# Turning the activated rows by DMA instead of TensorE, and a changed order for the last token tiles, in a fused attention and two-layer mixture kernel

## The chip, the cores and the metric

The kernel runs on one core of a Trainium2 chip. Five engines work in parallel, each through its own instructions in a fixed order: TensorE (PE, matmuls and transposes; its weight loads are listed apart as PEld), VectorE (DVE), ScalarE (ACT), GpSimd (POOL), and SyncE (SP), which here only issues DMAs. PE writes to PSUM; DVE and ACT read PSUM, POOL does not. The metric is the time of one execution in microseconds on the device; less is better.

## What is computed

Three stages, one after the other, on 1152 tokens (2 sequences of 576) of 512 features:

```python
scores = q @ k.T / 8                        # 2 x 8 heads, 576 x 576
mask = scores >= (32nd largest of the row)  # others to -1e9
x = softmax(scores) @ v                     # -> [1152, 512]
xn = x / rms(x) * rms_g
x = (silu(xn @ w_gate) * (xn @ w_val)) @ w_out         # d_ff 1536
logits = x @ r_gate; e = argmax(logits); gate = softmax(logits)[e]
# token i takes the next free slot of expert e (288 slots each, 8 experts)
out[i] = gate * (relu(x[i] @ w1[e]) @ w2[e])           # F2 = 1024
```

## The kernel before

**Number format.** Matmuls of the second and third stage run in f16 with both operands split into an upper and a lower half (value = hi + lo); each product is three matmuls: hi·hi, hi·lo, lo·hi.

**Tiles.** Tokens go in nine tiles of 128 (`t` = 0 to 8), heads in pairs, so there are 36 pairs of work `p = 4t + hp`. For each pair `scores` makes the scores (L308), `topk` finds the 32nd largest with four MAX8 and three MATCH_REPLACE8 per head on DVE (L322, L331, L334), `weights` makes the softmax's numerators (ACT L350, L356, POOL L351) and `values` turns them and multiplies by v (L374, L382). After a tile's four pairs come `norm` (the rms norm, result `xn` as two f16 halves), `moe1` (the first feed-forward layer) and `dispatch` (routing and scatter of the row).

**moe1(t).** It runs over three groups g of 512 hidden features. Two products of 12 matmuls (L448) give gate and value; from these ACT and, for tiles 1 to 7, POOL make the activated rows `h` [128 tokens x 512] in f32 (L461 to L468). `turned(g, h)` then turns h: four transposes on PE into a PSUM buffer (L434), and `halves` splits that into the tile `hT[g]`, the upper half by ACT (L420) and the lower by DVE (L421). Groups 0 and 1 are turned after the first row chunk of the next group, group 2 after the fourth of the twelve row chunks (f = 0 to 11) of the down product (L473), whose chunks f = 8 to 11 read `hT[2]`.

**dispatch(t).** y, the layer's result, is turned (L492), copied by ACT (L494) and multiplied by the router's weights (L505). DVE, ACT and POOL find the expert and the slot (`ev` is the engine of four small steps: DVE for tile 8, else POOL). ACT squares y for a scale (L499) with the buffer `yd` as scratch; `yd` (one buffer) also takes the row that an indirect DMA of POOL writes to `disp` in DRAM (L568).

**Experts.** Weights (16 matrices of 2 MB) are loaded by SP (L722), sized (`size`, ACT L735) and split into halves (`convert`: ACT L760, DVE L762 and L765). Rows of an expert are fetched from `disp` by a transposing DMA (`gather`, L776) with their notes (L789). Expert 0 begins with the first 128 slots ("a") and takes up to 48 more ("b") later. Three weight loads stand behind the last of the first gathers on SP.

**Order.** The program is written by an outer loop of slots: each pair is 14 slots, and generators (`at`, `ahead`) are advanced at given slots. Scores, weights, values and norm have a raised priority; moe1 and dispatch have none. A scheduler then fixes each engine's order from priorities and modelled times, so each engine's order is static at run time. `after(t, engine)` puts the instructions traced in its block behind a remembered instruction, on that instruction's engine only. Two buffer pools matter: `wraw` (four buffers of 4 KB per partition, for raw weights and a row of zeros, all before 165 us), and `pm` (three PSUM banks, shared by the products and by the turned rows).

Of the kernel before, what the change touches and what calls it, by code (L numbers as in the profile page):

```python
# [8 lines left out]
F32 = mybir.dt.float32  # L9
F32R = mybir.dt.float32r  # L10
F16 = mybir.dt.float16
BF16 = mybir.dt.bfloat16
I32 = mybir.dt.int32
U32 = mybir.dt.uint32
AF = mybir.ActivationFunctionType
OP = mybir.AluOpType
PSUM = bass.MemoryType.PSUM

P = 128
B, H, S, D = 2, 8, 576, 64  # L20
N = B * S
DM = H * D
# [3 lines left out]
NT = N // P  # L26
HALF = S // 2
KC = DM // P
# [17 lines left out]
def tile_topk_attention__then__moe__then__moe_routed(  # L46
# [3 lines left out]
    nc = tc.nc  # L50
# [33 lines left out]
    def half(i, lo):  # L84
        return wbig[:, i, :].bitcast(F16)[:, lo * DM:(lo + 1) * DM]

    mx = ctx.enter_context(tc.tile_pool(name="mx", bufs=1))
# [6 lines left out]
    att = tc.alloc_tile_pool(name="att", bufs=2)  # L94
# [4 lines left out]
    for b in (6, 0, 1, 2, 3, 4, 5):  # L99
        c = 0  # L100
# [3 lines left out]
    wraw = {}  # L104
# [23 lines left out]
    def pow2_below_rsqrt(out, back, x, by, t):  # L128

        nc.gpsimd.tensor_scalar(t[:, 0:1], x, by, TINY, op0=OP.mult, op1=OP.add)  # L130
        nc.gpsimd.tensor_tensor(t[:, 1:2], t[:, 0:1], mhalf, op=OP.pow)
        yield
        exponent(out, t[:, 1:2])
        invert(back, out)
# [283 lines left out]

    def halves(out, x):
        nc.scalar.activation(out[:, :KC], x, AF.Copy)  # L420
        nc.vector.tensor_tensor(out[:, KC:], x, out[:, :KC], op=OP.subtract)  # L421

    yx = {}

    late = []

    def moe1(t, ew):
        hT = [mx.tile([P, 2 * KC, P], F16, name="hT", bufs=3) for _ in range(3)]
        xn = xnT.pop(t)

        def turned(g, h):
            tp = pm.tile([P, 4, P], F32, name="pm")
            for i in range(4):
                nc.tensor.transpose(tp[:, i, :], h[:, i * P:(i + 1) * P], ident)  # L434
            halves(hT[g], tp)

        h = None
        for g in range(3):
            th = mx.tile([P, DM], F32, name="th")
            if ew is nc.gpsimd:  # L440
                gs = mx.tile([P, DM], F32, name="gs")
            for w in range(2):
                b = 2 * g + w
                a = late[0].tile([P, DM], F32, name="late") if late and b % 3 else pm.tile([P, DM], F32, name="pm")
                for c in range(KC):
                    i = KC * b + c
                    for n, (x, lo) in enumerate(((0, 0), (0, 1), (KC, 0))):
                        nc.tensor.matmul(a, xn[:, x + c, :], half(i, lo), start=(c == 0 and n == 0), stop=(c == KC - 1 and n == 2))  # L448
                    if c == 1:
                        yield  # L450
                    if c == 0 and w == 0 and h is not None:
                        turned(g - 1, h)
                yield
                if w == 0 and ew is nc.vector:
                    nc.scalar.activation(th, a, AF.Tanh, scale=gdec[:, g:g + 1])
                    nc.vector.scalar_tensor_tensor(th, th, 1.0, a, op0=OP.add, op1=OP.mult)
                elif ew is nc.vector:
                    h = mx.tile([P, DM], F32, name="gs")
                    nc.vector.scalar_tensor_tensor(h, a, vg[:, g:g + 1], th, op0=OP.mult, op1=OP.mult)
                elif w == 0:  # L460
                    nc.scalar.activation(th, a, AF.Tanh, scale=gdec[:, g:g + 1])  # L461
                    nc.scalar.activation(gs, a, AF.Copy, scale=gdec[:, g:g + 1])
                    ew.tensor_tensor(th, th, gs, op=OP.mult)
                    ew.tensor_tensor(th, th, gs, op=OP.add)
                else:
                    h = mx.tile([P, DM], F32, name="gs")
                    nc.scalar.activation(h, a, AF.Copy, scale=vdec[:, g:g + 1])
                    ew.tensor_tensor(h, th, h, op=OP.mult)  # L468
        yps = pm.tile([P, DM], F32, name="pm")
        for f in range(NF1):  # L470
            i = 6 * KC + f
            for n, (hi, lo) in enumerate(((0, 0), (0, 1), (1, 0))):
                nc.tensor.matmul(yps, hT[f // KC][:, KC * hi + f % KC, :], half(i, lo), start=(f == 0 and n == 0), stop=(f == NF1 - 1 and n == 2))  # L473
            if f == 3:
                turned(2, h)
            if f % 2 == 1:
                yield
        yx[t] = route.tile([P, DM], F32, name="yx")
        nc.scalar.activation(yx[t], yps, AF.Copy, scale=ydec)
        yield  # L480

    scat, behind = [], {}

    def after(t, engine):

        return tc.issue_after(behind[t, engine].ins)

    def dispatch(t):
        y = yx.pop(t)
        yt = px.tile([P, KC, P], F32, name="px")  # L490
        for c in range(KC):
            nc.tensor.transpose(yt[:, c, :], y[:, c * P:(c + 1) * P], ident)  # L492
        yT = mx.tile([P, KC, P], F32, name="xu")
        nc.scalar.activation(yT, yt, AF.Copy)  # L494
        yd = mx.tile([P, ROW], F32, name="yd")
        yh, yl = (yd[:, i * DM // 2:(i + 1) * DM // 2].bitcast(F16) for i in range(2))
        nc.gpsimd.tensor_copy(yd[:, DM + 1:ROW], tok[:, t:t + 1])
        yn = route.tile([P, 8], F32, name="yn")
        nc.scalar.activation(yd[:, :DM // 2].bitcast(BF16), y, AF.Square, accum_out=yn[:, 0:1])  # L499
        size = iter(()) if t == NT - 1 else pow2_below_rsqrt(yn[:, 1:2], yn[:, 2:3], yn[:, 0:1], 1.01, yn[:, 3:5])  # L500
        next(size, None)
        yield
# [27 lines left out]
        nm = route.tile([P, 4], F32, name="nm")  # L530
# [7 lines left out]
        nc.vector.max(k8, key)  # L538
        yield
        oh = route.tile([P, E], BF16, name="oh")  # L540
        ev = nc.vector if t == NT - 1 else nc.gpsimd
        ev.tensor_scalar(oh, rank8, k8[:, 0:1], None, op0=OP.is_equal)
        if t == NT - 1:
            nc.tensor.matmul(lp[:, 2, :], ones16, cum, start=True, stop=True)
# [6 lines left out]
        nc.vector.tensor_scalar(nm[:, 2:3], nm[:, 1:2], EPSD, None, op0=OP.add)  # L551
        yield
        nc.vector.scalar_tensor_tensor(scr, lp[:, 1, :], 1.0, oh, op0=OP.mult, op1=OP.mult, accum_out=pos[:, 0:1])
        behind[t, "dve"] = nc.vector.reciprocal(nm[:, 3:4], nm[:, 2:3])
        yield
        ev.tensor_scalar(pos[:, 2:3], pos[:, 0:1], float(cap), NOWHERE, op0=OP.is_ge, op1=OP.mult)
        ev.tensor_scalar(yd[:, DM:DM + 1], nm[:, 3:4], yn[:, 2:3], 1.0 / YS, op0=OP.mult, op1=OP.mult)
# [1 line left out]
        if t == NT - 1:  # L559
            nc.vector.tensor_scalar(had, lp[:, 2, 0:1], float(WA), None, op0=OP.min)  # L560
            nc.vector.tensor_scalar(rest, had, tok[:, 0:1], cap - 1.0, op0=OP.add, op1=OP.min)
            with after(t, "act"):
                gather("a", 0, 0, WA, ew, nc.scalar)
                notes("a", 0, 0, WA, ew, nc.scalar)
        slot = route.tile([P, 1], I32, name="slot")
# [3 lines left out]
            out=disp, out_offset=bass.IndirectOffsetOnAxis(ap=slot[:, :1], axis=0),  # L569
            in_=yd, in_offset=None, bounds_check=E * cap - 1, oob_is_err=False))  # L570
# [72 lines left out]
    for p in range(NP):  # L643
        t, hp = divmod(p, 4)
# [12 lines left out]
    for t in range(NT):  # L657
        ew = nc.vector if t in (0, 8) else nc.gpsimd
# [29 lines left out]
    ew = ctx.enter_context(tc.tile_pool(name="ew", bufs=1, reuse_waits="tile"))  # L688
# [64 lines left out]
    def convert(j, n):  # L753

        raw, (hi, lo), sc = raw_of(n), place(j), sized.pop(j)
        k = 4 if n < 4 else 2
        for g in range(k):
            r = slice(g * 2 * BIG // k, (g + 1) * 2 * BIG // k)
            if 2 * g < k:
                nc.scalar.activation(hi[:, r], raw[:, r], AF.Copy, scale=sc[:, 7:8])  # L760
            else:
                nc.vector.tensor_scalar(hi[:, r], raw[:, r], sc[:, 7:8], None, op0=OP.mult)  # L762
        for g in range(k):
            r = slice(g * 2 * BIG // k, (g + 1) * 2 * BIG // k)
            nc.vector.scalar_tensor_tensor(lo[:, r], raw[:, r], sc[:, 7:8], hi[:, r], op0=OP.mult, op1=OP.subtract)  # L765
# [5 lines left out]
    def gather(k, e, lo, hi, pool, eng):  # L771

        r = e * cap + lo
        n = -(-(hi - lo) // 16) * 16
        xgT[k] = pool.tile([P, 2 * KC, n], F16, name="xgT", bufs=1 if pool is ew else 3)
        g = eng.dma_start_transpose(out=xgT[k], in_=disp.bitcast(F16)[r:r + n, :2 * DM])  # L776
        return g

    def notes(k, e, lo, hi, pool, eng):

        for i, (o, m) in enumerate(chunks(hi - lo)):
            x = pool.tile([P, E, 2], F32, name=f"notes{i}", bufs=1 if pool is ew else 2)
            if k == 1 and not lo:
                eng.dma_start(x[:m, 1:], disp[:E * cap].rearrange("(e c) d -> c e d", c=cap)[lo + o:lo + o + m, 1:, DM:])
                every[i] = x
                for f in range(1, E):
                    meta[f, i] = x[:, f]
            else:
                eng.dma_start(x[:m, e], disp[e * cap + lo + o:e * cap + lo + o + m, DM:])  # L789
                meta[k, i] = x[:, e]  # L790
# [22 lines left out]
    convert(0, 0)  # L813
    size(2, 2)
    convert(1, 1)
    with after(NT - 2, "dve"):
        convert(2, 2)
    fetch_w()
    size(3, 3)
# [75 lines left out]

    with after(NT - 1, "pe"):
        up("a", 0, WA)
    convert(3, 3)
    last = gather(1, 1, 0, W, eb, nc.sync)
    rest_gather()  # L900
    notes(1, 1, 0, W, eb, nc.sync)
# [113 lines left out]
```

## Time and profile before

| what | value |
|---|---|
| median of 3 timed runs | 703.59 us (702.87 to 703.71) |
| the profiled execution | 701.31 us, span 699.4 us |
| PE busy | 556.6 us (80%) |
| DVE busy | 611.0 us (87%) |
| ACT busy | 496.7 us (71%) |
| POOL busy | 439.3 us (63%) |
| mean granted clock of PE | 0.921 |

The profile is of one execution; times count from its first instruction. A row of the window view gives a stretch (start:end), its length, then for PE, PEld, DVE, ACT and POOL the busy us with the number of instructions in brackets, then the granted clock of PE (1.00 is 2.4 GHz, 0.50 is 1.2 GHz), the busy share of the DMA engines, and GB/s. A row of the timeline gives start, duration, engine, line, operation, output and input with the number of merged instructions, and in square brackets the engine's idle time before it and what ended it. A row of the groups gives line, engine, operation, shapes, count, then busy us and mean ns of one, then idle time before. A line of the chain of waits gives start, us and what held the end up. A matmul's or a vector instruction's duration overlaps its successor's; the distance of two starts is what one costs in a row of them.

### The profile page before, as it was taken

The numbers are of one execution on the slowest core, as the hardware profiler recorded it, in microseconds if no ns is written. First come the engines' busy times: TensorE is split into PE (matmuls) and PEld (weight loads), VectorE is DVE, ScalarE is ACT, GpSimd is POOL, SyncE is SP. The second block draws the span as 40 slices with busy tenths as digits, with TensorE's granted clock in tenths as the row PEclk, the third lists the DMA queues.
The fourth block names the chain that finished last, engine by engine and source line by source line (L and its number), as shares of the span: only waits on it lengthen the run. The fifth ranks groups of instructions, "written<-read, shape, count | busy, mean of one in ns | idle before, by whom it ended". The sixth has DMA issues, their size and how long they took to land.

```text
span 699.4 us, 12982 instructions
## 1 busy us (share of the span) xinstructions
PE 556.6 (80%) x4708; PEld 403.0 (58%) x4708; DVE 611.0 (87%) x1215; ACT 496.7 (71%) x959; POOL 439.3 (63%) x521
## 2 busy tenths in 40 slices
PE   1216424468687999999999999999999489999994
PEld 1115413334454666766667665665644289999994
DVE  3999999999999999999999999995169646999950
ACT  3456548579966888888788887887697338899711
POOL 3795889989895978876978779596613210111412
PEclk9999555588889999999999999999999679999998
DMA  8999171384000001000000000002820479999101
GB/s 220 247 346 304 37 226 45 122 263 155 15 8 17 9 30 51 10 31 16 24 9 31 16 15 16 1 17 89 316 94 0 150 151 397 323 346 319 48 21 39
DMA packets 47016, 80.00 MB, mean 114 GB/s; under 512 B 18732, under 2 KB 23340, under 8 KB 46946
## 3 DMA queue, kind: packets, MB, share of 16 engines
q1 hardware_dynamic: 43954, 74.02, 34.0%
q0 software_dynamic: 1792, 4.83, 1.8%
q8 instruction: 39, 0.64, 0.4%
q10 hardware_dynamic: 1200, 0.26, 0.2%
q14 instruction: 31, 0.25, 0.1%
HBM read 64.35 MB, written 12.27 MB: 110 GB/s over the span
## 4 chain that ended last, share of the span: by engine, by line
DVE 26%; PE 24%; issue 20%; POOL 13%; DMA 10%; ACT 4%; SPq 2%; POOLq 0%; ACTq 0%; DVEq 0%
PE pm L448 8%; DVE r L331 7%; DVE m L334 6%; PE pm L473 5%; DMA vt<-in_v_l_dram 3%; PE xps L382 3%; DMA wbig<-in_w_out_dram 3%; POOL pp L351 3%; DVE wbig L157 3%; POOL out_dram L890 3%; DVE m L322 2%; DVE wbig L155 2%; PE tp L374 2%; DVE wbig L226 2%; PE tp L308 2%
## 5 line engine op out<-in xcount | busy, mean ns | idle before, releaser
L448 PE MATMUL pm<-wbig,xn 128*128 128x512 f16 x600 | 153.8, 388 | 7.1 <-ACT xn L420 3.5
L334 DVE MAX8 m<-r 128x8 f32<-128x576 f32 x216 | 156.7, 744 | 0.4
L848 PEld LDWEIGHTS <-split 128*128 128x128 f16 x1728 | 117.6, 100 | 8.7 <-issue 8.5
L308 PE MATMUL tp<-kst,qh 128*128 128x288 f32 (+1 forms) x160 | 64.5, 415 | 64.8 <-ACT s L310 20.9
L351 POOL TENSOR_TENSOR pp<-s,pp 128x576 f32<-128x576 f32 x72 | 102.8, 1440 | 10.1 <-ACT pp L350 9.5
L331 DVE MATCH_REPLACE8 r<-m,r 128x576 f32<-128x576 f32 x144 | 106.2, 740 | 0.0
L448 PEld LDWEIGHTS <-xn 128*128 128x128 f16 x648 | 63.2, 100 | 72.6 <-issue 12.8
L473 PE MATMUL pm<-wbig,hT 128*128 128x512 f16 x324 | 79.9, 389 | 9.6 <-DVE wbig L226 4.3
L308 PEld LDWEIGHTS tp<-kst,qh 128*128 128x128 f32 (+1 forms) x160 | 32.7, 206 | 89.9 <-ACT s L310 28.6
L310 ACT ACTIVATE s<-tp 128x288 f32<-128x288 f32 x144 | 54.6, 410 | 19.8 <-POOL pp L351 16.4
L765 DVE SCALAR_TENSOR_TENSOR split<-raw,sc,split 128x2048 f16<-128x2048 f32 (+1 forms) x32 | 65.8, 2077 | 0.9 <-ACT split L760 0.8
L374 PE MATMUL tp<-ident,pp 128*128 128x128 f32 x324 | 56.8, 294 | 11.2 <-ACT pp L356 10.8
L890 POOL DMA_INDIRECT out_dram<-ob,tos x14 | 19.4, 1388 | 73.5 <-ACT ob L888 71.7
L350 ACT ACTIVATE pp<-s,bias 128x576 f32<-128x576 f32 x72 | 51.9, 772 | 16.5 <-POOL bias L336 16.3
L848 PE MATMUL acc<-xgT,split 128*128 128x168 f16 (+1 forms) x768 | 58.8, 240 | 5.1 <-DMA xgT<-disp 2.7
L848 PE MATMUL acc<-hE,split 128*128 128x168 f16 (+2 forms) x864 | 60.1, 232 | 2.5 <-DVE hE L859 1.9
L735 ACT ACTIVATE junk<-raw 128x2048 bf16<-128x2048 f32 (+1 forms) x32 | 54.1, 1692 | 10.3 <-DMA raw<-in_w_dram 7.1
L356 ACT ACTIVATE pp<-pp,bias 128x576 f32<-128x576 f32 x72 | 56.3, 782 | 3.2 <-POOL pp L351 2.8
L375 ACT ACTIVATE pt<-tp 128x384 f32<-128x384 f32 x108 | 48.7, 492 | 11.8 <-PE tp L374 7.0
L374 PEld LDWEIGHTS tp<-ident,pp 128*128 128x128 f32 x324 | 41.3, 150 | 25.8 <-ACT pp L356 14.1
L382 PE MATMUL xps<-pt,vt 128*64 128x128 f32 (+1 forms) x800 | 55.6, 279 | 0.0
L322 DVE MAX8 m<-s 128x8 f32<-128x576 f32 x72 | 53.6, 745 | 0.9 <-ACT s L310 0.7
(201 smaller groups left out, 1234.7 us busy)
## 6 DMA issues: line engine op xcount, KB each, us to landing
raw<-in_w_dram SPq DMA_DIRECT2D x28, 1024.0 KB, 8.5
wbig<-in_w_out_dram SPq DMA_DIRECT2D x6, 1024.0 KB, 9.0
disp<-wraw SPq DMA_DIRECT2D x18, 257.0 KB, 5.7
qraw<-in_q_l_dram SPq DMA_DIRECT2D x72, 64.0 KB, 2.2
wraw<-in_w_gate_dram SPq DMA_DIRECT2D x8, 512.0 KB, 4.5
split<-in_w_dram SPq DMA_DIRECT2D x4, 1024.0 KB, 7.6
kraw<-in_k_l_dram SPq DMA_DIRECT2D x12, 288.0 KB, 4.3
wbig<-in_w_val_dram SPq DMA_DIRECT2D x3, 1024.0 KB, 7.6
```

The costliest lines, as they stand in the source:

```text
L308: nc.tensor.matmul(sp[:c1], x[:, i, :c1], kst[b, hp][:, i, c * HALF:(c + 1) * HALF], start=(n == 0), stop=(n == 1))
L322: nc.vector.max(m[:, i, 0], s[i])
L331: nc.vector.match_replace(r[i], m[:, i, n - 1], src, -3.0e38)
L334: nc.vector.max(m[:, i, n], r[i])
L351: nc.gpsimd.tensor_tensor(w, s[i], w, op=OP.subtract)
L356: nc.scalar.activation(pp[p][:, i], pp[p][:, i], AF.Exp, bias=bias[:, i, 0:1], scale=0.125, accum_out=sums[t][:, h:h + 1])
L374: nc.tensor.transpose(tp[:, i, :], p2[:, o:o + P], ident)
L382: nc.tensor.matmul(xps[t][rows, hp, c0:c1], v, w, start=(n == 0), stop=(n == 4))
L448: nc.tensor.matmul(a, xn[:, x + c, :], half(i, lo), start=(c == 0 and n == 0), stop=(c == KC - 1 and n == 2))
L473: nc.tensor.matmul(yps, hT[f // KC][:, KC * hi + f % KC, :], half(i, lo), start=(f == 0 and n == 0), stop=(f == NF1 - 1 and n == 2))
L765: nc.vector.scalar_tensor_tensor(lo[:, r], raw[:, r], sc[:, 7:8], hi[:, r], op0=OP.mult, op1=OP.subtract)
L848: nc.tensor.matmul(a, u[:, c, col * P:(col + 1) * P], v[:, c, :a.shape[-1]], start=(c == 0 and n == 0), stop=(c == nk - 1 and n == 2))
```

## The change

For tiles 1 to 6 `turned` no longer uses PE. ACT writes the upper half of `h` as it stands into a `wraw` buffer, POOL (`ew`) the lower half beside it, and one transposing DMA of SP ([128 x 1024] f16, SBUF to SBUF) fills `hT[g]`. It is called as soon as h is there. Tiles 0, 7 and 8 keep the old way. For the last tiles: `behind[t, "dve"]` now remembers the last lower half of hT, and the conversions of weights 2 and 3 stand behind that of tile 8 (weight 2 stood behind a step of tile 7's routing, weight 3 behind nothing); the four small routing steps of tile 7 go to DVE; the square of tile 8 uses a buffer `th` as scratch; and the first gather stands behind ACT's copy of the turned y of tile 8, not behind its exponential.

```diff
     def halves(out, x):
         nc.scalar.activation(out[:, :KC], x, AF.Copy)
-        nc.vector.tensor_tensor(out[:, KC:], x, out[:, :KC], op=OP.subtract)
+        return nc.vector.tensor_tensor(out[:, KC:], x, out[:, :KC], op=OP.subtract)
...
         def turned(g, h):
+            if 0 < t < NT - 2:
+                hs = att.tile([P, 1, 2 * DM], I32, name="wraw", bufs=4).rearrange("p a f -> p (a f)")[:, :DM].bitcast(F16)
+                nc.scalar.activation(hs[:, :DM], h, AF.Copy)
+                ew.tensor_tensor(hs[:, DM:], h, hs[:, :DM], op=OP.subtract)
+                nc.sync.dma_start_transpose(out=hT[g], in_=hs)
+                return
             tp = pm.tile([P, 4, P], F32, name="pm")
...
-            halves(hT[g], tp)
+            behind[t, "dve"] = halves(hT[g], tp)
...
-                    if c == 0 and w == 0 and h is not None:
+                    if c == 0 and w == 0 and h is not None and not 0 < t < NT - 2:
                         turned(g - 1, h)
...
                     ew.tensor_tensor(h, th, h, op=OP.mult)
+                    if t < NT - 2:
+                        turned(g, h)
...
-            if f == 3:
+            if f == 3 and not 0 < t < NT - 2:
                 turned(2, h)
...
-        nc.scalar.activation(yT, yt, AF.Copy)
+        behind[t, "xu"] = nc.scalar.activation(yT, yt, AF.Copy)
...
-        nc.scalar.activation(yd[:, :DM // 2].bitcast(BF16), y, AF.Square, accum_out=yn[:, 0:1])
+        sq = yd[:, :DM // 2] if t < NT - 1 else mx.tile([P, DM], F32, name="th")[:, :DM // 2]
+        nc.scalar.activation(sq.bitcast(BF16), y, AF.Square, accum_out=yn[:, 0:1])
...
-        ev = nc.vector if t == NT - 1 else nc.gpsimd
+        ev = nc.vector if t >= NT - 2 else nc.gpsimd
...
-        behind[t, "dve"] = nc.vector.reciprocal(nm[:, 3:4], nm[:, 2:3])
+        nc.vector.reciprocal(nm[:, 3:4], nm[:, 2:3])
...
-            with after(t, "act"):
+            with after(t, "xu"):
                 gather("a", 0, 0, WA, ew, nc.scalar)
...
-    with after(NT - 2, "dve"):
+    with after(NT - 1, "dve"):
         convert(2, 2)
...
-    convert(3, 3)
+    with after(NT - 1, "dve"):
+        convert(3, 3)
```

## Rows read from the trace of the kernel before

**Rows 1.** Windows, columns as told above.
```profile
255.00:305.00 50.00, 48.43 (x380) 33.84 (x380) 49.91 (x110) 42.42 (x94) 41.76 (x52) 1.00 0.11 32
480.00:540.00 60.00, 58.46 (x348) 32.18 (x347) 31.64 (x76) 48.71 (x91) 24.14 (x35) 1.00 0.40 145
205.00:475.00 270.00, 258.53 (x1852) 169.68 (x1851) 268.59 (x600) 220.87 (x502) 214.31 (x281) 1.00 0.06 20
553.00:560.00 7.00, 2.82 (x17) 2.60 (x18) 3.21 (x23) 3.23 (x5) 1.03 (x2) 0.50 0.18 38
600.00:650.00 50.00, 49.58 (x680) 49.19 (x678) 48.65 (x79) 45.29 (x50) 9.52 (x6) 1.00 1.02 322
```

**Rows 2.** Timeline of DVE: a turn among top-k passes, and the last pass.
```profile
237.42 0.68 DVE L421 TENSOR_TENSOR hT<-pm,hT 128x512 f16<-128x512 f32 x1
238.02 0.75 DVE L334 MAX8 m<-r 128x8 f32<-128x576 f32 x1
...
479.49 0.76 DVE L334 MAX8 m<-r 128x8 f32<-128x576 f32 x1
```

**Rows 3.** Timelines of the engines and queues between 540 and 561 us.
```profile
543.36 0.68 DVE L421 TENSOR_TENSOR hT<-pm,hT 128x512 f16<-128x512 f32 x1
544.10 4.02 PE L473 MATMUL pm<-wbig,hT 128*128 128x512 f16 x10 [3.59 <-DVE sc L744]
545.79 4.87 DVE L765 SCALAR_TENSOR_TENSOR split<-raw,sc,split 128x1024 f16<-128x1024 f32 x4
552.26 0.63 ACT L499 ACTIVATE yd<-yx 128x512 bf16<-128x512 f32 x1 [3.42 <-DMA disp<-yd,slot]
553.52 1.88 PE L505 MATMUL px<-rg,xu 128*128 128x8 f32 x8 [3.97 <-ACT xu L494]
556.21 1.36 ACTq L776 DMA_TRANSPOSE xgT<-disp  x1
560.63 1.06 POOL L568 DMA_INDIRECT disp<-yd,slot  x1 [3.00 <-ACT junk L735]
```

**Rows 4.** Chain of waits, between 543 and 560 us.
```profile
543.82 8.34 DMA disp<-yd,slot
...
557.60 2.23 DMA notes<-disp
```

**Rows 5.** PE's transposes: group from 255 to 480 us, then two neighbours.
```profile
L434 PE MATMUL pm<-ident,gs 128*128 128x128 f32 x64 | 14.0, 278 | 0.1
...
494.18 0.27 PE L434 MATMUL pm<-ident,gs 128*128 128x128 f32 x1
494.29 0.59 PE L448 MATMUL pm<-wbig,xn 128*128 128x512 f16 x2
```

**Rows 6.** Groups by form: the nearest operations on POOL and ACT.
```profile
L525 POOL TENSOR_TENSOR yd<-yx,yd 128x512 f16<-128x512 f32 x8 | 9.3, 1161 | 12.3 <-ACT yd L524 12.1
L524 ACT ACTIVATE yd<-yx 128x512 f16<-128x512 f32 x8 | 5.1, 640 | 0.0
```

**Rows 7.** DMA issues: count, median us from issue to landing.
```profile
disp<-yd,slot POOLq DMA_INDIRECT x9, 3.3
xgT<-disp ACTq DMA_TRANSPOSE x1, 3.2
xbT<-xb SPq DMA_TRANSPOSE x1, 2.7
```

**Rows 8.** All transposing gathers together (tile xgT).
```profile
DMA to landing us min/median/max: 3.2/5.6/12.7
```

**Rows 9.** Timeline of POOL and PE around one tile's third turn.
```profile
431.88 1.28 POOL L468 TENSOR_TENSOR gs<-th,gs 128x512 f32<-128x512 f32 x1
433.12 2.78 POOL L351 TENSOR_TENSOR pp<-s,pp 128x576 f32<-128x576 f32 x2
438.25 0.60 PE L473 MATMUL pm<-wbig,hT 128*128 128x512 f16 x2
```

**Rows 10.** The slot computation on POOL: ns, least, median, most.
```profile
L566 POOL TENSOR_SCALAR slot<-pos x8: 376/380/2337, 243.1 to 541.2; 128x1 int32<-128x1 f32 x8
```

More of the change, by code (lines that the diff above doesn't have):

```diff
@@ L420, in halves, with after @@
         nc.scalar.activation(out[:, :KC], x, AF.Copy)
-        nc.vector.tensor_tensor(out[:, KC:], x, out[:, :KC], op=OP.subtract)
-    yx = {}
-    late = []
+        return nc.vector.tensor_tensor(out[:, KC:], x, out[:, :KC], op=OP.subtract)
+    yx, late, behind = {}, [], {}
+    def after(t, engine):
+        return tc.issue_after(behind[t, engine].ins)
     def moe1(t, ew):
@@ L480, in moe1 @@
         yield
-    scat, behind = [], {}
-    def after(t, engine):
-        return tc.issue_after(behind[t, engine].ins)
+    scat = []
     def dispatch(t):
```

## The prediction, made before the changed kernel was run

> **What bounds the kernel now.** I read the table of windows first, then the timelines of PE and DVE, then the chain of waits at the end. From 255 to 540 us PE is busy almost without a gap (48.43 of 50 us in the first window, 58.46 of 60 in the last), at the full granted clock, while up to 475 us DVE is as full (268.59 of 270) [rows 1]. So two engines are at their limit together: DVE runs the top-k passes and ends the last at 480.2 us [rows 2]; PE is behind with the first feed-forward stage, whose matmuls come last in priority, and works off its arrears from 480 to 540 us, when DVE is only half busy. What ends that stretch late is therefore PE's sum of work, not DVE's. POOL has 214.31 of 270 us and ACT 220.87 [rows 1]: neither is the limit, but neither is idle.
>
> From 540 to 563 us nothing is full. The chain of waits shows a string of stalls: DVE converts expert weights (L762, L765) ahead of the last lower half of hT, PE waits 3.59 us for that, the scatter of tile 7 takes 8.34 us to land, ACT waits 3.42 us for it, and the scatter of tile 8 waits for a gather and its notes [rows 3, 4]. From 600 to 650 us PE has 49.58 of 50 us and DMA is full too [rows 1]: the experts' stage keeps its length, and it moves with its start and with the weight loads, which queue on SP behind the gathers.
>
> **Part 1: 18 turns (tiles 1 to 6, three each) leave PE and DVE.**
> Removed on PE: 72 transposes. Eight of them lie before 255 us, where PE has gaps; the 64 after [rows 5] count. Busy time (278 ns) overlaps; the cadence is what one costs: a transpose starts at 494.18 and the next matmul at 494.29, 0.11 us [rows 5]. 64 x 0.11 = 7.0 us out of the engine that ends the stretch.
> Removed on DVE: 18 subtractions, start to start 0.60 us (237.42 to 238.02) [rows 2]: 10.8 us. The last top-k would end at about 469. That gain alone does not reach the end, since PE is still behind; it leaves PE more arrears and no less work. I count 7.0, not 10.8.
> ACT: the copy of the upper half now reads SBUF instead of PSUM; the row of that kind is 640 ns [rows 6]. Even if all of it were new, 18 x 0.64 = 11.5 us would fit into the 49 that ACT has free in 270 [rows 1]; I take 0.
> POOL: 18 subtractions 128x512 f16 from f32; the trace has that shape at 1161 ns [rows 6]: 20.9 us, so 235.2 of what would be 259 us, 91% instead of 79%. The top-k chain on POOL (bias, then two L351) has the higher priority, so the feed-forward's products bear the delay.
> SP: 18 transposing DMAs of 128x1024 f16. Nearest rows: a gather of the same size, beside little else, landed 3.2 us after issue; one of 48 rows out of SBUF took 2.7; the slowest, larger and from DRAM beside weight loads, 12.7 [rows 7, 8]. DMA share between 205 and 475 us is 0.06 [rows 1], so I take 3.2 and keep 2.7 and 12.7 as ends. SP now waits for POOL ahead of each; queued behind are the q loads. A load stands 5 of a pair's 14 slots ahead of its split, some 4 us; I cost it at 0, and if POOL is late by more, ACT waits at the split and the scores behind it.
> The new wait is on the third turn of a tile, needed by the ninth row chunk of the down product. In the row of one tile h is ready at 433.16, PE comes to that chunk at 438.25 [rows 9]. New chain: 0.64 (ACT) + 1.16 (POOL) + 3.2 (DMA) = 5.0 us, ready at 438.2, just in time; with the pair of L351 in front on POOL (to 435.9) it is ready at 440.2, 2 us late. Behind that matmul in PE's order stand scores and values. Between 0 and 2 I take 0.5 a tile, 3.0 us for six; the ends are 0 and 12 at 3.2 us a DMA.
> Sum of part 1: -7.0 + 3.0 = **-4.0 us** (-7 to +5).
>
> The Trainium skill has a rule against this part: its page "VectorE: DVE Perf Modes", section "The three transpose paths", gives 1309 ns for a 128x128 block by DMA and 390 by TensorE, and its rules say to use TensorE where PSUM will do. An estimate from that page is 8 x 1.31 = 10.5 us a DMA; the sum would then be the slower rival's below. The gather's 3.2 us for eight blocks [rows 7] speaks against adding the blocks up; no row shows one of 128 partitions out of SBUF.
>
> **Part 2: order at the end.** All in the times of the trace before; part 1 shifts them as a whole.
> (a) The conversions of weights 2 and 3 stand behind the last lower half of hT on DVE. That half then runs when ACT has its upper half, at about 539.7 instead of 543.36, and PE passes at 540.5 to its last ten matmuls without the 3.59 us wait, at 0.22 instead of 0.40 us each (4.02 us for ten, after the gap) [rows 3]. Saves 3.6 + 1.9 = 5.5.
> (b) The square of tile 8 goes to another buffer, so ACT does not wait 3.42 us for tile 7's scatter, and the copy of the turned y is next: 3.1 us. The eight L505 took 1.88 us [rows 3] in a stretch whose granted clock was 0.50 [rows 1], the lower of its two levels, 1.2 GHz, with PE mostly idle before; at 2.4 GHz they take 0.9: 1.0. The logits are there at about 546, not 555.4: 9.4 in all.
> (c) Tile 7's slot on DVE: on POOL that one instruction took 2.34 us beside DVE's conversions, against a median of 0.38 [rows 10]. Its scatter starts some 5 us earlier and before the weight load, so at about the 3.3 us median [rows 7] it has landed by 542 to 543 and bounds nothing.
> (d) What is paid back: both conversions (2 x 6.1 us of DVE; four of the six pieces of one are the 4.87 us at 545.79 [rows 3], the other two 1.3) now lie from 540.3 to 552.5, in tile 8's routing. That chain took 2.9 us; it meets DVE at about four places, each up to one 1.2 us piece: +3, from 0 to +6.6 if all pieces go first.
> (e) The first gather goes behind the copy of the turned y (545.4) instead of behind the exponential (issued 556.21 [rows 3], landed 559.4): about 548.7, 10.7 earlier. The scatter of tile 8, which waited 2.3 us for that gather's notes [rows 4], waits no more: 558.3 becomes 549 + 3 = 552, issue at 552 against 560.63 [rows 3], 8.7 earlier; the gathers and weight loads behind it on SP follow it.
> (f) The load that waits for conversion 2 starts 3 us later than before against its own stretch; four slots are full by then, no cost.
> PE's start gains 10.7, the loads 8.7; both are full afterwards, so I take the smaller, rounded: **-9 us** (-4 to -11).
>
> **Sum.** The profiled execution took 701.31 us (span 699.4 and 1.9 around it). 701.3 - 4 - 9 = 688.3. The median of the timed runs is 703.59, 2.3 above; forecast 688.3 + 2.3 = 690.6, rounded to **690**.
>
> **Rivals.**
> 1. *Only the end gains.* POOL at 91% and the DMA wait eat the 7 us; the experts still start 9 earlier: 703.6 - 9 = 694.6. For it: POOL's waits on ACT and the stretch where h, the norm and the routing come together. Against: the work added to POOL is not in the top-k chain, and PE's arrears hide lateness. Chance 0.17.
> 2. *Only the middle gains.* The conversions stand whole before tile 8's routing: (d) at 6.6 and a few DVE waits for ACT behind it: the end gains 3 to 4, the whole 703.6 - 4 - 3.5 = 696. For it: DVE runs in a fixed order, and the trace shows routing steps standing behind L765 pieces. Chance 0.10.
> 3. *More.* No wait at the ninth chunk and (d) small: 703.6 - 7 - 11 = 685.6, and if DVE's 10.8 count too, 682. Chance 0.15.
> 4. *Slower.* PE stands at the ninth chunk for each of six tiles because the DMA is slow to land. With 12.7 us, the longest row, the chain takes 14.5 us; PE covers 5.1, so 9.4 a tile, 56 for six, less 7 and 9: 744. It decides from a landing time of about 5.9 us (wait 2.7 a tile, 16 for six, which eats both gains). By the estimate from the Trainium skill's page above, 10.5, it would be 7.2 a tile, 703.6 + 43 - 16 = 731. Against: DMA is idle there. Chance 0.08.
> 5. *The change does not do what it says* (the turns still wait for PE, or the order is what it was): 703 to 705. Chance 0.02.
> The forecast itself, 687 to 693, holds 0.48.
>
> **How the numbers follow.** Range 680 to 700: it holds the forecast, rivals 1 to 3, and leaves out 4, 5 and a little of the edges. No change is what lies within 0.2% (1.4 us), about the spread of this kernel's runs. Faster: forecast and rivals 1 to 3, 0.90, less 0.01 for tails that reach 702: 0.89. Same 0.03, slower 0.08.
>
> **What would show it.** Right: no L434 between 240 and 480 us and 18 DMA transposes landing in about 3 us; last top-k near 469; L473's last matmuls end near 539; no ACT wait of L499 on the scatter; first expert matmul near 546, span near 686. Wrong: PE waiting on DMA hT over 2.7 us a tile; DVE waiting for s; POOL over 95% before 470; routing of tile 8 behind all eight L765.

## The result, and the profile after

The changed kernel took 709.92 us (median of 7 runs, 707.57 to 712.22), the kernel before 703.71 beside it (7 runs): ratio 1.0088, 95% interval 1.0070 to 1.0107. The forecast was 690. The profiled execution took 709.8 us, its span 707.8.

The windows of the kernel after, in the columns of [rows 1]:

```profile
255.00:305.00 50.00, 49.38 (x348) 32.20 (x346) 45.04 (x98) 39.73 (x87) 44.18 (x50) 0.99 0.18 44
480.00:540.00 60.00, 53.72 (x333) 29.98 (x332) 25.20 (x63) 46.72 (x89) 29.30 (x41) 1.00 0.42 154
205.00:475.00 270.00, 250.97 (x1731) 159.44 (x1729) 254.18 (x563) 215.83 (x487) 223.41 (x281) 0.98 0.14 34
```

Work did leave the two full engines: between 205 and 475 us PE is busy 250.97 us and DVE 254.18, 7.6 and 14.4 less than in [rows 1]. Not all of that is gone. PE ran 121 matmuls fewer there, and only 68 of them are transposes for turns; nearly all of the other 53 ran later. Over the whole execution PE is busy 1.7 us less (554.9) and DVE 7.6 (603.4). The transposes in that stretch of the kernel before, with least, median and longest ns (after has none there):

```profile
L434 PE MATMUL pm<-ident,gs x68: 270/273/329, 233.0 to 469.1; 128*128 128x128 f32 x68
```

And nothing ended earlier. DVE's last top-k pass, which ended at 480.2 [rows 2], ends later:

```profile
485.48 0.76 DVE L334 MAX8 m<-r 128x8 f32<-128x576 f32 x1
```

The view of waits says what DVE did instead: which engine and line waited, for whom, us in total, times, longest. First the kernel after (205 to 486 us), then the kernel before (205 to 480):

```profile
DVE m L322 <- ACT s L310: 6.0, 10, 1.3
DVE lg L515 <- PE px L512: 4.1, 1, 4.1
DVE scr L560 <- PE px L553: 1.7, 1, 1.7
```

```profile
DVE m L322 <- ACT s L310: 0.7, 1, 0.7
DVE yn L137 <- POOL yn L131: 0.3, 1, 0.3
```

Before, DVE practically never waited, so it looked like a bound that any relief would shorten. After, it waits for scores (`s`) and for one routing step of an early tile. The 4.1 us are one instruction, with everything behind it in line; first DVE, then PE in the kernel after:

```profile
327.73 0.17 DVE L515 COPY lg<-px 128x8 f32<-128x8 f32 x1 [4.08 <-PE px L512]
...
325.31 1.39 PE L382 MATMUL xps<-pt,vt 128*64 128x64 f32 x40
326.63 1.06 PE L512 MATMUL px<-rg,xu 128*128 128x8 f32 x8
```

The copy of eight logits stands in DVE's line ahead of passes that need nothing from it, while PE still works off other matmuls ahead of L512. PE tells the same; its waits in the kernel after, 205 to 486 us:

```profile
PE tp L308 <- ACT pt L375: 6.1, 4, 3.0
PE pm L456 <- ACT xn L420: 4.6, 3, 2.2
PE pm L483 <- DMA hT<-wraw: 3.4, 6, 1.0
```

The new wait for the DMA is there and is small: 3.4 us in all. The transposing DMAs themselves, all 18 (tile hT):

```profile
DMA to landing us min/median/max: 3.0/3.0/3.2
```

At the end, in the stretch of [rows 3], DVE of the kernel after:

```profile
552.68 1.28 DVE L421 TENSOR_TENSOR hT<-pm,hT 128x512 f16<-128x512 f32 x2
...
555.20 2.47 DVE L772 SCALAR_TENSOR_TENSOR split<-raw,sc,split 128x1024 f16<-128x1024 f32 x2
...
558.91 7.26 DVE L772 SCALAR_TENSOR_TENSOR split<-raw,sc,split 128x1024 f16<-128x1024 f32 x6
...
566.15 0.15 DVE L515 COPY lg<-px 128x8 f32<-128x8 f32 x1
...
570.69 0.17 DVE L560 SCALAR_TENSOR_TENSOR scr<-px,oh 128x8 f32<-128x8 f32 x1 [2.71 <-PE px L553]
...
571.10 0.27 DVE L573 TENSOR_SCALAR slot<-pos 128x1 int32<-128x1 f32 x1
```

The last lower halves have no conversion ahead of them any more, as foreseen; but all eight conversion pieces (L772) now stand ahead of tile 8's logits, whose matmuls had ended at 562.8. The routing then waits another 2.7 us for a matmul (L553) that stands on PE behind 62 matmuls of the first expert. The scatter of tile 8 goes out at 572.80, not 560.63 [rows 3], and the up to 48 further rows "b" of expert 0 (tile xbT) are fetched behind that scatter. PE waits for them, which it did not before; PE of the kernel after:

```profile
583.29 3.85 PE L855 MATMUL acc<-xbT,split 128*128 128x48 f16 x96 [4.17 <-DMA xbT<-xb]
```

### The profile page after: what moved, and what is told of

It reads as the page before. It is cut to its first block, busy times and chain, and to the rows that moved or that the text cites. A ratio compares the mean times of both kernels' runs of the same rounds, so it can differ in the third digit from the quotient of the medians.

```text
span 707.8 us, 12869 instructions
## 1 busy us (share of the span) xinstructions
PE 554.9 (78%) x4636; PEld 395.6 (56%) x4636; DVE 603.4 (85%) x1202; ACT 498.5 (70%) x959; POOL 456.2 (64%) x534
## 4 chain that ended last, share of the span: by engine, by line
DVE 30%; PE 19%; issue 15%; ACT 14%; POOL 12%; DMA 7%; SPq 1%; POOLq 0%; ACTq 0%; DVEq 0%
DVE r L331 7%; DVE m L334 7%; PE pm L456 6%; PE pm L483 4%; DVE wbig L155 4%; DVE wbig L157 3%; DVE m L322 3%; ACT junk L742 3%; PE xps L382 2%; POOL pp L351 2%; ACT pp L350 2%; DVE wbig L226 2%; PE tp L308 2%; POOL out_dram L897 2%; DMA hT<-wraw 2%
## 5 line engine op out<-in xcount | busy, mean ns | idle before, releaser
L456 PE MATMUL pm<-wbig,xn 128*128 128x512 f16 x600 | 148.2, 388 | 9.3 <-ACT xn L420 4.6
L456 PEld LDWEIGHTS <-xn 128*128 128x128 f16 x648 | 62.8, 100 | 80.5 <-issue 14.4
L374 PE MATMUL tp<-ident,pp 128*128 128x128 f32 x324 | 57.3, 297 | 11.5 <-ACT pp L356 10.7
L772 DVE SCALAR_TENSOR_TENSOR split<-raw,sc,split 128x2048 f16<-128x2048 f32 (+1 forms) x32 | 65.8, 2079 | 0.1
L382 PE MATMUL xps<-pt,vt 128*64 128x128 f32 (+1 forms) x800 | 58.0, 277 | 1.4 <-ACT pt L375 1.4
```

Of the source, the lines that this page charges most:

```text
L374: nc.tensor.transpose(tp[:, i, :], p2[:, o:o + P], ident)
L382: nc.tensor.matmul(xps[t][rows, hp, c0:c1], v, w, start=(n == 0), stop=(n == 4))
```

## The experiments

Theories: **S**, any new set of instructions gets another fixed order from the scheduler, and engines then stand in line behind steps that come late; **P**, POOL's extra work delays softmax and scores; **E**, the end's new order costs.

All runs in one table. Ratio: to the kernel before, on the same chip, with its 95% interval. Then, from the profiled execution, in us: end of the last top-k pass, start of ACT's copy of tile 8's y out of PSUM, first expert matmul, and from there to the end of the span (the experts' stage). Last column: whether DVE's instructions follow one another as before.

| kernel | ratio | last pass | y of 8 | first expert | to the end | DVE order |
|---|---|---|---|---|---|---|
| before | 1 | 480.2 | 548.2 | 559.4 | 140.0 | - |
| after | 1.0088 (1.0070-1.0107) | 486.2 | 559.7 | 564.4 | 143.4 | another |
| m_only | 1.0306 (1.0283-1.0329) | 486.3 | 563.5 | 574.5 | 149.6 | another |
| t_only | 1.0083 (1.0053-1.0112) | 481.1 | 543.9 | 561.1 | 144.8 | another |
| m_dve | 1.0213 (1.0162-1.0265) | 496.4 | 553.5 | 571.8 | 144.6 | another |
| p_dummy | 1.0227 (1.0195-1.0260) | 489.7 | 563.1 | 574.1 | 147.0 | another |
| m_hi | 1.0108 (1.0088-1.0128) | 485.2 | 556.1 | 567.8 | 139.4 | another |
| b_nosub | 1.0165 (1.0142-1.0187) | 477.3 | 556.5 | 563.8 | 148.4 | another |
| n_tiny | 1.0184 (1.0156-1.0213) | 478.5 | 550.9 | 562.7 | 145.2 | another |
| n_one | 0.9998 (0.9973-1.0023) | 483.9 | 552.3 | 563.1 | 140.0 | as before |
| n_dve | 1.0145 (1.0122-1.0169) | 481.2 | 553.5 | 566.5 | 147.4 | another |
| a_prio | 1.0213 (1.0178-1.0247) | 487.9 | 557.6 | 574.3 | 140.8 | another |
| t_late | 1.0181 (1.0160-1.0203) | 478.4 | 541.2 | 546.3 | 164.2 | another |
| a_late | 1.0399 (1.0361-1.0436) | 488.9 | 562.3 | 567.2 | 164.3 | another |
| t_best | 1.0060 (1.0038-1.0083) | 482.3 | 546.2 | 555.4 | 152.3 | another |
| a_best | 1.0235 (1.0205-1.0265) | 488.9 | 562.5 | 571.2 | 151.2 | another |
| t_best2 | 0.9968 (0.9948-0.9987) | 481.7 | 544.4 | 549.5 | 149.5 | another |

One profiled execution is no median. n_one has the order of before on DVE and the same time, and its landmarks still lie 4 us later, so a difference of that size in one column means nothing alone. The distances between landmarks say more: from the last pass to the first expert matmul it is 79.2 us in both, from there to the end 140.0 in both. The profiled execution of n_tiny took 709.7 us, 5 us less than the median of its runs.

### Halves of the change

**m_only**: the 18 turns by DMA, the end as before (`turned` of the change, called behind h; nothing of the rest).

> Only the turns of tiles 1 to 6 go by DMA; the end keeps its old order. Theory S (static order: with the new instructions each engine's fixed order is another one, and DVE and PE stand in line behind steps that are late on the chip): slower than before by 4 to 9 us, since nothing of the end's change is needed for the loss. Theory P (POOL's 21 us more at 85 to 90% load delay the softmax, the scores and DVE): the same 4 to 9 us, with DVE's waits for s as the whole of it. Rival E (the end's new order is what costs): no slower than before, 0 to -7 us.

**t_only**: the end's new order, all turns by PE.

```
-            if 0 < t < NT - 2:
...
-                nc.sync.dma_start_transpose(out=hT[g], in_=hs)
-                return
...
```

> Only the changes of order for the last tiles; all turns by PE. Theories S and P: the loss is not here; -2 to -6 us against before, because the scatter of tile 7 and the square no longer hold tile 8, less what the eight conversion pieces ahead of tile 8's routing pay back. Rival E: slower by 3 to 9 us.

Measured: the DMA turns alone cost 3.1%, the end alone 0.8%, both together 0.9%. The 21 us that m_only loses are far more than the 4 to 9 of S and P. The 5 us or so that t_only loses are in the range of E, where S and P had a gain. The halves don't add: the end's edits give back most of what the turns lose, and lose on the kernel whose middle is intact. m_only's middle is that of the kernel after. Why t_only's experts start no earlier shows in one place (the larger part of its loss, 4.8 us, lies in the experts' stage, see below); DVE, then POOL of t_only:

```profile
546.53 4.86 DVE L764 SCALAR_TENSOR_TENSOR split<-raw,sc,split 128x1024 f16<-128x1024 f32 x4
...
553.82 0.15 DVE L507 COPY lg<-px 128x8 f32<-128x8 f32 x1
553.90 0.26 DVE L565 TENSOR_SCALAR slot<-pos 128x1 int32<-128x1 f32 x1
...
554.96 1.09 POOL L567 DMA_INDIRECT disp<-yd,slot  x1 [13.70 <-DVE yn L517]
```

This is the slot of tile **7**, moved to DVE to make its scatter early: it stands behind all conversions. Its scatter goes out at 554.96, against 543.82 [rows 4], and the first gather, which needs it, at 557.85, against 556.21 [rows 3].

### Is it POOL?

**m_dve**: m_only with the 18 subtractions on DVE.

```
-                ew.tensor_tensor(hs[:, DM:], h, hs[:, :DM], op=OP.subtract)
+                nc.vector.tensor_tensor(hs[:, DM:], h, hs[:, :DM], op=OP.subtract)
```

> As m_only, but the lower half of the 18 rows is subtracted by DVE instead of POOL (18 x 0.6 us back on DVE, 21 us off POOL). Theory P: 4 us or more faster than m_only, DVE's waits for s back near 1 us. Theory S: no fixed sign against m_only, within 4 us of it, with waits of another kind in the place of those removed.

**p_dummy**: the kernel before, with 18 subtractions of that shape on POOL whose result nobody reads.

```
...
+                        ew.tensor_tensor(hs[:, DM:], h, th, op=OP.subtract)
```

> The kernel before, with 18 more subtractions 128x512 to f16 on POOL in tiles 1 to 6 whose result nobody reads; turns stay with PE and DVE. Theory P: slower than before by 4 us or more, with DVE waiting for s. Theory S: within 2 us of before, since nothing else hangs on them.

**m_hi**: DMA turns without the split; POOL writes the upper half, the lower half of h is left out.

```
...
+                    ew.tensor_tensor(hs[:, :DM], th, h, op=OP.mult)
+                    nc.sync.dma_start_transpose(out=hT[g][:, :KC], in_=hs[:, :DM])
...
```

> The 18 turns by DMA on the order of before for the end, without the split: POOL writes the product straight as the upper half (no copy on ACT, no subtraction on POOL or DVE, half the DMA), and the product with the lower half takes the upper one again; the lower half of h is left out. P (POOL's 21 us more delay softmax and scores): POOL's load is that of before, so DVE's idle time between 205 us and the last pass falls under 4 us and the last pass ends near 470, first expert matmul near 550. S (the fixed order changes and DVE and PE stand in line): idle stays at 8 us or more, the last pass ends between 478 and 486, first expert matmul after 560.

**n_tiny**: p_dummy with one element a partition in place of 512.

> The kernel before with 18 more instructions on POOL of one element a partition, whose result nobody reads: no load (18 x some 0.2 us), but another fixed order. P: as before, 703 to 706 us, last pass 480 +-2. S: the new order alone costs: last pass 483 to 490, 708 us or more.

Measured: p_dummy, 2.3% slower, fits P; S had no loss there. m_dve, without POOL's load, is 6.8 us faster than m_only by the medians (719.02 to 725.83 us), as P had it and beyond the 4 of S; but the waits for scores, which P had near 1 us, are 7.3. That its last pass ends later still (496.4) tells little, since DVE has its 10.8 us of subtractions back. m_hi has no extra POOL work, and DVE waits most of all for scores; and n_tiny, 18 instructions with no load, costs 1.8%. DVE's waits in m_hi, 205 to 485 us, then the largest in m_dve, 205 to 496:

```profile
DVE m L322 <- ACT s L310: 10.6, 16, 1.6
DVE rs L391 <- POOL rs L389: 1.2, 2, 1.0
```

```profile
DVE m L322 <- ACT s L310: 7.3, 10, 2.3
```

P alone does not explain the middle, and it is not excluded: p_dummy's last pass ends 11 us after that of n_tiny, which has the same instructions at one element (and another order). n_tiny missed S's numbers too: its last pass is not late, it loses after that.

### Relief without anything added

**b_nosub**: the kernel before with DVE's 18 subtractions taken out and nothing put elsewhere (the lower half of h is left out for tiles 1 to 6).

```
-            halves(hT[g], tp)
+            if 0 < t < NT - 2:
+                nc.scalar.activation(hT[g][:, :KC], tp, AF.Copy)
...
```

> The kernel before with its turns on PE, but the lower half of h for tiles 1 to 6 left out (upper half taken twice): DVE loses 18 subtractions (10.8 us), nothing goes to POOL or to a DMA. If DVE alone sets the middle: last pass near 469, idle under 3 us. S (scores come just in time; what DVE is given back it waits): idle 8 us or more, last pass 476 to 486, and the time 702 or more.

Measured: 10.8 us less work on DVE, last pass 2.9 us earlier, and the kernel 1.65% **slower**. DVE's waits rise to 7.2 us, 3.7 of them for scores. So what DVE is given back, it mostly waits; and what ends earlier in the middle is lost behind it. Idle time came out just under the 8 that S named.

**a_prio**: the whole change, the early tiles' routing at the priority of the top-k steps.

```
-        ... ahead(dispatch(t), 0) ...
+        ... ahead(dispatch(t), 200 if t < NT - 2 else 0) ...
```

> The whole change, with the routing of tiles 0 to 6 at the priority of the top-k steps instead of the lowest: its matmuls no longer stand behind the feed-forward's. S: DVE's waits for PE px (5.8 us after the change) fall under 2, but the new order brings others: last pass 480 to 488. If these waits were the cause of the late middle: last pass 480 or less and the time 704 or less.

Measured: the 4.1 us wait for L512 is gone, waits for scores and others stay at 11.9 us in all (13.7 after the change), the last pass ends at 487.9 and the kernel is 2.1% slower. Removing a wait by its name brought another order with others.

### One empty instruction

**n_one** and **n_dve** add one instruction of one element a partition to the kernel before.

```
+                    if (t, g) == (1, 0):   # n_one, on POOL;   n_dve: (4, 1), nc.vector
...
+                        ew.tensor_tensor(hs[:, DM:DM + 1], h[:, :1], th[:, :1], op=OP.subtract)
```

> The kernel before with one more POOL instruction of one element a partition (tile 1, first gate group), result unused. The fixed order of DVE and SP is that of before, ACT and POOL differ at two or three places. S: time as before within 0.3%, last pass 480 +-2, first expert matmul 559 +-2. If an added instruction costs by itself, or if kernels differ by a per cent without any cause in the order: 706 or more, or 700 or less.

> The kernel before with one more DVE instruction of one element a partition (tile 4, second gate group), result unused: 0.1 us of work, but the fixed order of DVE differs from before at 481 places and that of ACT at 342. S: a time other than before's by 0.5% or more, likely slower (706 to 715), with first expert matmul or the experts' stage (140 us before) longer. If order does not matter: within 0.3% of before.

Measured: n_one, whose DVE and SP lists keep their order, takes the time of before (0.9998). n_dve, some 0.1 us of work, moves DVE's list at 481 places and costs 1.45%. So the order alone is worth more than a per cent here. Its last pass is at 481.2; the loss lies behind it, from there to the first expert matmul (85.3 us against 79.2) and in the experts' stage (+7.4), though no line of that stage differs. What differs there is PE's order; PE before, then in n_dve:

```profile
570.39 6.42 PE L848 MATMUL acc<-hE,split 128*128 128x128 f16 x83 [1.95 <-DVE hE L859]
576.65 2.59 PE L848 MATMUL acc<-xbT,split 128*128 128x48 f16 x96
```

```profile
578.46 1.22 PE L851 MATMUL acc<-xbT,split 128*128 128x48 f16 x26 [4.02 <-DMA xbT<-xb]
579.50 6.63 PE L851 MATMUL acc<-hE,split 128*128 128x128 f16 x83
```

Before, the second product of expert 0 (hE) runs whole and the rows "b" (xbT) come behind it. In n_dve 26 matmuls of "b" stand ahead of the last 83 of hE, which need nothing from them, and PE waits for the fetch of "b". The same split after 12 or 13 matmuls is in every kernel with the experts' code of before whose stage takes 144.6 to 149.6 us (m_only, t_only, m_dve, p_dummy, b_nosub, n_tiny, n_dve; PE waits 0.6 to 4.2 us for xbT), and in none that takes 139.4 to 140.8 (before, n_one, m_hi, a_prio). The stage's windows, before and n_dve:

```profile
559.40:699.40 140.00, 126.28 (x1817) 124.46 (x1816) 98.66 (x162) 89.40 (x100) 24.35 (x18) 0.95 0.66 205
566.50:713.90 147.40, 129.16 (x1817) 127.17 (x1816) 99.43 (x163) 89.97 (x100) 26.24 (x18) 0.93 0.62 195
```

Of the 7.4 us, 4.5 are more idle time of PE; the other 2.9 are more time in which it is busy with the same 1817 matmuls, at a granted clock of 0.93 in place of 0.95.

For the middle the order alone is not shown as the cause. n_tiny and n_dve, which add next to no work, end the last pass at 478.5 and 481.2. It is late with DMA turns (m_hi 485.2, m_only 486.3) and with POOL's load on the old turns (p_dummy 489.7).

### The end

**t_late**, and **a_late** on the whole change: conversions 2 and 3 and the first send behind tile 8's slot step.

```
-        ev.tensor_scalar(slot, ...)
+        behind[t, "dve"] = ev.tensor_scalar(slot, ...)
...
+    with after(NT - 1, "dve"):
+        send("a", WA, True)
```

> The end's new order alone (turns by PE as before), but the conversions of weights 2 and 3 stand on DVE behind the slot step of tile 8 instead of behind the last lower half of hT, and the first send behind it too. E (the end is late because tile 8's logits copy and tile 7's slot step stand on DVE behind eight conversion pieces): logits copy of tile 8 at about 548 us instead of 553.8, slot of tile 7 near 543 instead of 553.9, scatter of tile 8 near 553 instead of 562.4, first expert matmul near 552 instead of 561.1; time 695 to 699. If the end is late for another reason (the weights' loads, or the order of the experts' stage): 704 to 709, first expert matmul still after 558.

> The whole change with the same two steps put behind tile 8's slot step. E: the middle stays as after the change (last top-k pass 486 +-2), tile 8's logits copy about 8 us earlier against its y, scatter of tile 8 near 565 instead of 572.8; time 700 to 704. If the end's order does not matter: 708 to 712.

Measured: E is right on where the start of t_late went and wrong on the time; a_late, at 731.96 us, is far behind both forecasts (700 to 704, 708 to 712). In t_late the experts start at 546.3, 13 us earlier than before, and from there to the end it takes 164 us instead of 140. PE, then SP of t_late:

```profile
546.29 3.04 PE L847 MATMUL acc<-xgT,split 128*128 128x128 f16 x27 [1.52 <-DMA xgT<-disp]
560.60 1.44 PE L847 MATMUL acc<-hE,split 128*128 128x128 f16 x12 [5.90 <-DVE hE L858]
...
555.92 0.44 SPq L721 DMA_DIRECT2D raw<-in_w_dram  x1
567.00 17.95 SPq L721 DMA_DIRECT2D raw<-in_w_dram  x9
```

Load 4 waits for the buffer that conversion 2 reads: its halves go out at 555.92 and 567.00, not at 542.25 as before, and PE waits 13.8 us in all for lower halves that stand behind conversions.

**t_best**, **a_best**: load 4 in a buffer of its own; conversion 2, then the first product's lower halves, then conversion 3.

```
-        return raws[n % 2 if n < 4 else n % 4]
+        return raws[n % 2 if n < 4 else (n + 2) % 4]
...
+    with after(NT - 1, "slot"):
+        convert(2, 2)
+    with after(NT - 1, "up"):
+        convert(3, 3)
...
```

> The end's new order with the turns by PE, and on DVE: tile 8's routing to its slot step, conversion of weight 2, the two lower halves of the first product, conversion of weight 3. Load 4 goes into a buffer of its own and waits for no conversion. If t_late lost its early start (first expert matmul 546.3) because load 4 stood behind conversion 2 (SP 555.9 and 567.0 instead of 542.3) and because lower halves stood behind conversions (PE waited 13.8 us for hE): load 4 issues before 547, first expert matmul near 546, hE waits under 5 us, span 686 to 692, time 688 to 696, faster than the kernel before. If the experts' stage has another bound: 700 or more.

> The same end in the whole change (turns by DMA). The middle as after the change (last pass 486 to 489), so some 8 to 10 us behind t_best: 697 to 706. If the middle's lateness is covered by the end: within 2 us of t_best.

**t_best2**: t_best with load 4 behind the gathers, together with loads 5 to 7.

> t_best with load 4 issued behind the gathers together with loads 5 to 7, so nothing stands beside tile 7's scatter and the first gather. E (the early load cost t_best its early start): first expert matmul 545 to 548 again instead of 555.4, burst of loads from about 562 instead of 570, waits for hE of the first product under 3 us; time 692 to 700. If the experts' stage loses it all the same (conversions and lower halves in another fixed order): over 702, with waits for hE of 5 us or more after 600.

Measured: t_best keeps part of the start only; load 4 goes out at 546.18, and the first gather beside it lands at 555.3. t_best2 has neither load nor conversion in the way of the start, and beats the kernel before by 0.32% (0.13 to 0.52%), just over what can be told from no change. Its start is 10 us early and its stage 9.5 us longer; PE waits 3.5 us in one place, where it waited 1.9 before:

```profile
549.50 3.02 PE L844 MATMUL acc<-xgT,split 128*128 128x128 f16 x27 [1.52 <-DMA xgT<-disp]
...
560.03 6.19 PE L844 MATMUL acc<-hE,split 128*128 128x128 f16 x57 [3.54 <-DVE hE L855]
```

Of the times expected, t_best's came out on the rival's side (700 or more), a_best's behind both, and t_best2's, 700.74, between the two. a_best and a_late, with DMA turns, take 1.8 and 2.4% longer than their twins with PE turns (720.05 to 707.27 us, 731.96 to 714.86): these ends do not hide the middle. The change's own end does: with it the kernel after (1.0088) takes as long as t_only (1.0083).

## Why the prediction was wrong

**The step that failed** is the first of part 1: "64 x 0.11 = 7.0 us out of the engine that ends the stretch". It let every other step keep its place, and took work that leaves PE as time that the stretch ends earlier. But the order was made anew: from 205 us to the last pass PE's waits rose from 11 to 19 us and DVE's from 1 to 14, some 50 other matmuls moved behind 475 us, and the last pass came 6.0 us later instead of 11 earlier.

Two more terms failed. Part 2 had -9: from the last pass to the first expert matmul the kernel after takes 78.2 us against 79.2, and t_only, with the end alone, 80.0. And "the experts' stage keeps its length": it is 3.4 us longer, with the 4.2 us wait for the rows "b". In the profiled executions 6.0 - 1.0 + 3.4 = 8.4 us, where the forecast had -13.

No rival had this mechanism. The slower one had a 744 by a slow DMA, and that was a wrong place to look: the DMA landed in 3.0 us. Two of the signs of being wrong did come: DVE waits for s, and the routing of tile 8 stands behind all eight pieces.

- DMA 3.2 us taken, 3.0 measured: right. The waits for it, 3.0 taken and 3.4 measured, agree by luck: only two of the six, 1.8 us, are at the ninth row chunk; four, 1.7 us, are at the fifth, which the prediction left out. The estimate of 10.5 us from the Trainium skill, page "VectorE: DVE Perf Modes", section "The three transpose paths", would have been 3.5 times the measured 3.0: here the figure for one block does not multiply with the blocks of one transfer.
- POOL at 91% foreseen; it was 83% (223.41 of 270) in a stretch that ran late. What its load costs in the middle no run separates from the order.
- (a) Right: from the last pass to y of tile 8 it takes 62.8 us in t_only, 67.9 before and 68.3 in n_one: 5.1 less, against 5.5.
- (b) Right in the main: in t_only the logits' matmuls end at 547.5, 7.9 earlier, where 9.4 was foreseen; ACT no longer waits for the scatter.
- (c) Wrong: foreseen 5 us earlier, in t_only 11.1 later. The slot left an engine that is free for one whose line is full. In the kernel after it happened to stand ahead of the conversions, and its scatter went out at 553.56.
- (d) The end that rival 2 names came true: all pieces first. The wait for the logits is 6.3 us in t_only, against 3 taken and 6.6 as the bound. In the kernel after it is 3.3, and 2.7 for L553 come on top.
- (e) Against y of tile 8, the first gather left 1.4 us behind it after, 8.1 before. In m_only it is 7.4; the 5.9 us between are most of why the kernel after is 10 us ahead of m_only at the first expert matmul, an earlier y is the rest. Tile 8's scatter did not follow: 13.1 us behind y, 12.5 before. Nor did the burst of weight loads behind the gathers, foreseen 8.7 earlier: it starts at 583.4 against 571.5, 23.7 and 23.3 us behind y.
- (f) Wrong as a rule. A load that waits for a conversion is the head of the experts' stage: t_late, where its halves went out some 14 and 24 us later, lost 24 us there, though part of that is the lower halves.
- "PE's start gains 10.7, the loads 8.7; both are full afterwards": the experts' stage does not just move with its start. With its code unchanged it took 139.4 to 149.6 us in m_only, m_dve, p_dummy, m_hi, b_nosub, n_tiny and n_dve, against 140.0, by where the order puts the rows "b" on PE.

Open: what makes the middle late, the new order, POOL's load or the longer way of a turn over ACT, POOL and SP (p_dummy has the first two, 2.3%; n_tiny the first, 1.8%, and no late middle). No run pinned the old order under the new instructions.

## What to carry to other kernels

Where a scheduler writes one fixed order per engine, price an edit on a second line: what a new order costs or gives, measured with an empty instruction that moves the order (here 1.5%, more than the 0.9% of the whole change). An engine that never waits is not thereby the only bound: look at how close the next ones are, and treat work taken off it as waits until a trace shows the end moving. Before moving a small step to another engine, or a stage's start forward, read what stands ahead of it in that engine's line and which load waits behind it. When a stage whose code is untouched takes longer, compare the order of its instructions first.

## What was not expected of the hardware

A transposing DMA of 128x1024 f16 within SBUF took 3.0 us from issue to landing, at most 3.2 in 18 cases, about as long as the gather of the same size before (3.2 us [rows 7]). The granted clock fell in the middle, to 0.98 on the mean of the stretch of 270 us where it had been 1.00 [rows 1], with 19 us of waits on PE in place of 11, and in the experts' stage of n_dve to 0.93 from 0.95.
